# Moving the streamed tiles of two feed-forward layers to one place by the remainder of 512 bytes

## The chip, the cores and the metric

The kernel runs on one core of a Trainium2 chip. The metric is the device time of one execution in microseconds (us); the median of three runs stands for a kernel. TensorE does matrix products: a stationary operand of 128x128 words is loaded by a weight load (PEld in the profile), and then a moving operand, here called a stream, of up to 512 columns is sent through it by a matmul (PE). VectorE (DVE), ScalarE (ACT) and GpSimd (POOL) do the elementwise work, and SyncE (SP) issues the DMAs. SBUF is the working memory of 128 partitions; an address in this text is a byte offset inside a partition, the same in all of them.

## The reference

```python
def mab(q, kv):
    s = scale * (q @ kv.transpose(0, 2, 1))
    s = s - s.max(-1, keepdims=True)
    a = np.exp(s)
    a /= a.sum(-1, keepdims=True) + 1e-09
    return a @ kv
h = mab(I, x)                      # 32 inducing rows against 12480 tokens of 128
x = mab(x, h)
h = x @ w_in;  x = np.maximum(0.01 * h, h) @ w_out          # layer 1, d_ff 2048
h = x @ w_in2; x = (h / (1 + np.exp(-1.702 * h))) @ w_out2  # layer 2, d_ff 2048
```

Everything is float32: x is 12480x128, the weights are 128x2048 and 2048x128.

## The kernel before

The tokens are cut into 25 tiles: 23 of 512 tokens and, last in each layer, two of 352. Attention comes first, in about 45 us, with the weights' conversion beside it. Then `steps` (L799) runs layer 1 and layer 2, tile after tile, 16 steps to a tile; a step is one block of 128 of the 2048 hidden units. The order on each engine is the order in which the code issues the work (`manual_schedule`, L105); tokens of layer 2 follow those of layer 1 without a pause.

To keep float32 accuracy at the speed of the fp32r type, an operand is split into a high and a low half and the products are summed:

- `ffn_in`, layer 1 (L743): one matmul, stationary a 128-column slice of `hw`, stream `at`. Attention's last product is folded into `hw`, so that `at` holds the attention weights.
- `ffn_in`, layer 2 (L747 to L749): three matmuls, stationary slices of `w2h`, `w2l`, `w2h`, streams `x2h`, `x2h`, `x2l`.
- `ffn_act` (L757 to L765): the activation and the split of its result into `ghi` (ScalarE) and `glo` (VectorE). In layer 2 the Silu's result passes through a tile `g`.
- `ffn_out` (L775 to L777), both layers, three steps later (`LOOK`): three matmuls, stationary slices of `v1` or `v2`, streams `ghi`, `ghi`, `glo`. At a tile's end layer 1 adds one more, L779, with stationary `lin` and stream `at`.

So a step has 4 matmuls in layer 1 (65 to a tile, with L779) and 6 in layer 2 (96 to a tile), and each has a weight load of its own, which runs while the matmul ahead of it streams.

Where the tiles lie: the pools `const`, `slots`, `wts` and `conv` are allocated one after the other and stay; the pool `main` (L501) is opened where the pools of the attention were, and takes its tags in the order of their first use, each buffer rounded up to a multiple of 32 bytes. A first tile of `main`, `gap` (L505), is never written or read; it only takes room. In the program before, all the stationary operands of the layers (`hw`, `w2h`, `w2l`, `v1`, `v2`, `lin`, slices of 512 bytes) start at addresses that leave 416 when divided by 512. `main` starts at a remainder of 416 too, and behind `gap`'s 448 bytes and 5248 bytes of small tiles (`nmx`, `na`, `nsum`, `rows`) follow `at`, `ghi` and `glo`: 416 + 448 + 5248 leaves 480. Two tiles of 64 bytes (`mxt`, `sst`) and others of whole multiples of 512 lie between these and `x2h`, which so starts at 480 + 128, remainder 96:

| tile | operand of | remainder of 512, before | from the stationary operands' place |
|---|---|---|---|
| `hw`, `v1`, `v2`, `w2h`, `w2l`, `lin` | stationary | 416 | 0 |
| `at`, `ghi`, `glo` | stream | 480 | 64 above |
| `x2h`, `x2l` | stream, layer 2 alone | 96 | 192 above |
| `g`, `o_t` | no matmul | 96 | 192 above |

All buffers of the streams are 2048 bytes, a multiple of 512, so that every buffer of a tag has the same remainder.

Of the kernel before, what the change touches and what calls it, by code (L numbers as in the profile page):

```python
# [10 lines left out]
F32 = mybir.dt.float32  # L11
# [7 lines left out]
P = 128  # L19
# [38 lines left out]
def kernel(  # L58
# [442 lines left out]
    main = ctx.enter_context(tc.tile_pool(name="main", bufs=2))  # L501
    ps_a = ctx.enter_context(tc.tile_pool(name="ps_a", bufs=2, space=PSUM))


    main.tile([P, 112], F32, tag="gap", name="gap", bufs=1)  # L505

    def halves(src, name, pool=const, tag=None):
        shape = list(src.shape)
        hi = pool.tile(shape, F32R, name=f"{name}h", tag=f"{tag or name}h")
        lo = pool.tile(shape, F32R, name=f"{name}l", tag=f"{tag or name}l")  # L510
        nc.scalar.activation(out=hi, in_=src, func=AF.Copy)
        nc.vector.tensor_tensor(out=lo, in0=src, in1=hi.bitcast(F32), op=ALU.subtract)  # L512
        return hi, lo
# [333 lines left out]
    def late_matrix(make, src, name, args, first):  # L847
        def begin():
            late[name], parts = make(src, name, *args)
            for k, part in enumerate(parts):  # L850
                stages = convert_stages(*part)
                n = first + 16 * k
                at(n + 1, stages[0])
                for j, stage in enumerate(stages[1:]):
                    at(n + 6 + 4 * j - (n + 6) % 4 + 2, stage)
        at(first, begin)

    late_matrix(matrix_in, moe2_w_in, "w2", ["w"], 60)
    late_matrix(matrix_out, moe2_w_out, "v2", [], 160)

    def split_x2(t):
        x2h_t[t] = halves(x2_t.pop(t), "x2", main)

    for t in range(NT):
        at(NT * NF + (t - 1) * NF + 6, split_x2, t)
# [51 lines left out]
```

## Time and profile before

| what | us |
|---|---|
| median of 3 runs (972.02 to 972.75) | 972.42 |
| the profiled execution, by the clock of the runs | 971.38 |
| its span, first to last instruction | 969.2 |
| TensorE matmul busy | 957.5 |
| ScalarE busy | 783.6 |
| VectorE busy | 633.7 |

The profiled execution lies 1.04 us (0.1%) below the median, and 2.2 us of it lie outside the span. A matmul's record overlaps the next one's, so the busy share says how much of the time some matmul was in flight; how fast they follow one another is read from their starts. In the profile a line such as `acc<-ghi,v` names the tile written, then those read.

### The profile page before, as it was taken

The numbers are of one execution on the slowest core, as the hardware profiler recorded it, in microseconds if no ns is written. First come the engines' busy times: TensorE is split into PE (matmuls) and PEld (weight loads), VectorE is DVE, ScalarE is ACT, GpSimd is POOL, SyncE is SP. The second block draws the span as 40 slices with busy tenths as digits, with TensorE's granted clock in tenths as the row PEclk, the third lists the DMA queues.
The fourth block names the chain that finished last, engine by engine and source line by source line (L and its number), as shares of the span: only waits on it lengthen the run. The fifth ranks groups of instructions, "written<-read, shape, count | busy, mean of one in ns | idle before, by whom it ended". The sixth has DMA issues, their size and how long they took to land.

```text
span 969.2 us, 13231 instructions
## 1 busy us (share of the span) xinstructions
PE 957.5 (99%) x4590; PEld 781.5 (81%) x4590; DVE 633.7 (65%) x1008; ACT 783.6 (81%) x1359; POOL 51.3 (5%) x63
## 2 busy tenths in 40 slices
PE   9889999999999999999999999999999999999998
PEld 7568787887878878898888888888888888888888
DVE  4778788878878777765555555555555555555555
ACT  6566677777767666689999999999999999999997
POOL 1311110201101000000000000000000000000000
PEclk9999999999999999999999999999999999999999
DMA  9202120031000100000000000000000000000000
GB/s 341 100 0 55 34 66 23 7 94 32 23 22 4 30 12 19 8 2 11 12 12 11 12 11 12 11 23 12 11 11 12 12 11 11 12 11 23 12 12 16
DMA packets 15433, 27.90 MB, mean 29 GB/s; under 512 B 2358, under 2 KB 6998, under 8 KB 15366
## 3 DMA queue, kind: packets, MB, share of 16 engines
q1 hardware_dynamic: 15366, 27.06, 8.7%
q8 instruction: 36, 0.59, 0.3%
q14 instruction: 31, 0.25, 0.1%
HBM read 14.79 MB, written 6.39 MB: 22 GB/s over the span
## 4 chain that ended last, share of the span: by engine, by line
PE 97%; DVE 2%; ACT 1%; POOL 0%; issue 0%; ACTq 0%; DVEq 0%
PE acc L777 19%; PE acc L776 18%; PE acc L775 18%; PE h_ps L749 9%; PE h_ps L743 9%; PE h_ps L747 9%; PE h_ps L748 9%; PE xT_ps L280 1%; PE idle_ps L118 1%; PE s_ps L599 1%; PE acc L779 1%; ACT e_t L311 0%; PE s_ps L295 0%; DVE mx L299 0%; DVE pT_t L339 0%
## 5 line engine op out<-in xcount | busy, mean ns | idle before, releaser
L765 DVE TENSOR_TENSOR glo<-g,ghi 128x512 fp32r<-128x512 f32 (+1 forms) x400 | 271.7, 679 | 239.2 <-ACT ghi L764 226.4
L757 ACT ACTIVATE ghi<-h_ps 128x512 fp32r<-128x512 f32 (+1 forms) x400 | 233.2, 588 | 99.7 <-PE h_ps L743 97.5
L758 DVE SCALAR_TENSOR_TENSOR glo<-h_ps,ghi 128x512 fp32r<-128x512 f32 (+1 forms) x400 | 264.8, 675 | 72.3 <-ACT ghi L757 67.2
L777 PE MATMUL acc<-glo,v 128*128 128x512 f32 (+1 forms) x800 | 309.9, 387 | 0.0
L776 PE MATMUL acc<-ghi,v 128*128 128x512 f32 (+1 forms) x800 | 309.0, 386 | 0.0
L775 PE MATMUL acc<-ghi,v 128*128 128x512 f32 (+1 forms) x800 | 308.1, 385 | 0.0
L763 ACT ACTIVATE g<-h_ps 128x512 f32<-128x512 f32 (+1 forms) x400 | 235.0, 587 | 35.8 <-PE h_ps L749 0.5
L764 ACT ACTIVATE ghi<-g 128x512 fp32r<-128x512 f32 (+1 forms) x400 | 248.2, 620 | 12.7
L776 PEld LDWEIGHTS acc<-ghi,v 128*128 128x128 f32 x800 | 150.3, 188 | 32.6
L777 PEld LDWEIGHTS acc<-glo,v 128*128 128x128 f32 x800 | 150.3, 188 | 30.2 <-DVE glo L758 0.4
L775 PEld LDWEIGHTS acc<-ghi,v 128*128 128x128 f32 x800 | 150.3, 188 | 28.6 <-issue 0.2
L749 PE MATMUL h_ps<-x2l,w2h 128*128 128x512 f32 (+1 forms) x400 | 156.8, 392 | 0.0
L743 PE MATMUL h_ps<-at,hw 128*128 128x512 f32 (+1 forms) x400 | 156.4, 391 | 0.4 <-ACT at L579 0.4
L747 PE MATMUL h_ps<-x2h,w2h 128*128 128x512 f32 (+1 forms) x400 | 154.7, 387 | 0.0
L748 PE MATMUL h_ps<-x2h,w2l 128*128 128x512 f32 (+1 forms) x400 | 153.1, 383 | 0.0
L743 PEld LDWEIGHTS h_ps<-at,hw 128*128 128x128 f32 x400 | 75.1, 188 | 20.1 <-issue 4.7
L748 PEld LDWEIGHTS h_ps<-x2h,w2l 128*128 128x128 f32 x400 | 75.1, 188 | 16.2
L749 PEld LDWEIGHTS h_ps<-x2l,w2h 128*128 128x128 f32 x400 | 75.1, 188 | 15.5
L747 PEld LDWEIGHTS h_ps<-x2h,w2h 128*128 128x128 f32 x400 | 75.1, 188 | 15.5
L793 ACT ACTIVATE x<-acc 128x512 f32<-128x512 f32 (+1 forms) x25 | 14.7, 587 | 7.6 <-PE acc L779 7.6
L796 DVE TENSOR_SCALAR o_t<-acc 128x512 f32<-128x512 f32 (+1 forms) x25 | 16.8, 670 | 0.5 <-PE acc L777 0.5
L512 DVE TENSOR_TENSOR x2l<-x,x2h 128x512 fp32r<-128x512 f32 (+1 forms) x25 | 16.8, 671 | 0.0
(108 smaller groups left out, 314.2 us busy)
## 6 DMA issues: line engine op xcount, KB each, us to landing
out_dram<-o_t SPq DMA_DIRECT2D x23, 256.0 KB, 2.0
xn<-in_x_dram SPq DMA_DIRECT2D x11, 512.0 KB, 10.1
raw<-in_moe_w_in_dram SPq DMA_DIRECT2D x8, 512.0 KB, 8.9
raw<-in_moe_w_out_dram SPq DMA_DIRECT2D x8, 512.0 KB, 4.4
at<-hlhi SPq DMA_DIRECT2D x42, 64.0 KB, 2.0
at<-hllo SPq DMA_DIRECT2D x42, 64.0 KB, 2.0
xn<-in_x_dram SPq DMA_DIRECT2D x2, 176.0 KB
out_dram<-o_t SPq DMA_DIRECT2D x2, 176.0 KB, 1.8
```

Source lines behind the costliest of these rows:

```text
L743: nc.tensor.matmul(o, hw[:, cols], at_t[t], start=True, stop=True)
L747: nc.tensor.matmul(o, wh[:, cols], hi, start=True, stop=False)
L748: nc.tensor.matmul(o, wl[:, cols], hi, start=False, stop=False)
L749: nc.tensor.matmul(o, wh[:, cols], lo, start=False, stop=True)
L757: nc.scalar.activation(out=hi, in_=o, func=AF.Relu)
L758: nc.vector.scalar_tensor_tensor(out=lo, in0=o, scalar=0.0, in1=hi.bitcast(F32), op0=ALU.max, op1=ALU.subtract)
L763: nc.scalar.activation(out=g, in_=o, func=AF.Silu, scale=BETA)
L764: nc.scalar.activation(out=hi, in_=g, func=AF.Copy)
L765: nc.vector.tensor_tensor(out=lo, in0=g, in1=hi.bitcast(F32), op=ALU.subtract)
L775: nc.tensor.matmul(o, v[:, f, 0, :], hi, start=(f == 0), stop=False)
L776: nc.tensor.matmul(o, v[:, f, 1, :], hi, start=False, stop=False)
L777: nc.tensor.matmul(o, v[:, f, 0, :], lo, start=False, stop=end)
```

## The change

`gap` shrinks from 112 words of 4 bytes to 88, from 448 to 352 bytes: everything behind it in `main` moves down by 96 bytes. When layer 2's first tile is split (`split_x2`, ahead of the first use of `x2h`), a second tile `gap2` of 96 words (384 bytes) is taken, once; `x2h`, `x2l`, `g` and `o_t` are allocated behind it. No instruction uses either gap.

```diff
-    main.tile([P, 112], F32, tag="gap", name="gap", bufs=1)
+    main.tile([P, 88], F32, tag="gap", name="gap", bufs=1)
...
+    gaps = []
+
     def split_x2(t):
+        if not gaps:
+            gaps.append(main.tile([P, 96], F32, tag="gap2", name="gap2", bufs=1))
         x2h_t[t] = halves(x2_t.pop(t), "x2", main)
```

Remainders after: `at`, `ghi`, `glo` 480 - 96 = 384; `x2h`, `x2l`, `g`, `o_t` 96 - 96 + 384 = 384. The stationary operands lie in pools ahead of `main` and stay at 416, so every stream of both layers starts 32 bytes below them by the remainder of 512.

## Rows read from the trace of the kernel before

**Rows 1.** Page, busy time and share of the span by engine.
```profile
PE 957.5 (99%) x4590; PEld 781.5 (81%) x4590; DVE 633.7 (65%) x1008; ACT 783.6 (81%) x1359; POOL 51.3 (5%) x63
```
**Rows 2.** Page, granted TensorE clock over 40 slices, 9 is 90% or more.
```profile
PEclk9999999999999999999999999999999999999999
```
**Rows 3.** Page, the chain of work that ended last, by engine and line.
```profile
PE 97%; DVE 2%; ACT 1%; POOL 0%; issue 0%; ACTq 0%; DVEq 0%
PE acc L777 19%; PE acc L776 18%; PE acc L775 18%; PE h_ps L749 9%; PE h_ps L743 9%; PE h_ps L747 9%; PE h_ps L748 9%; PE xT_ps L280 1%; PE idle_ps L118 1%; PE s_ps L599 1%; PE acc L779 1%; ACT e_t L311 0%; PE s_ps L295 0%; DVE mx L299 0%; DVE pT_t L339 0%
```
**Rows 4.** Stages: us, then busy us by engine, PEclk, DMA share, GB/s.
```profile
105.00:345.00 240.00, 240.00 (x1058) 194.20 (x1057) 194.50 (x307) 170.00 (x294) 29.31 (x28) 1.00 0.13 33
404.00:429.00 25.00, 25.00 (x150) 24.16 (x149) 18.29 (x35) 19.39 (x40) 0.00 (x0) 1.00 0.00 1
430.00:932.00 502.00, 502.00 (x2185) 409.98 (x2184) 278.99 (x409) 455.36 (x753) 0.00 (x0) 1.00 0.03 12
```
**Rows 5.** Timeline of TensorE, layer 1, L779 of two tiles: start us, us.
```profile
148.72 0.39 PE L779 MATMUL acc<-at,lin 128*128 128x512 f32 x1
...
163.59 0.40 PE L779 MATMUL acc<-at,lin 128*128 128x512 f32 x1
```
**Rows 6.** Timeline of TensorE, layer 2, L747 56 steps apart.
```profile
640.09 0.39 PE L747 MATMUL h_ps<-x2h,w2h 128*128 128x512 f32 x1
...
717.37 0.39 PE L747 MATMUL h_ps<-x2h,w2h 128*128 128x512 f32 x1
```
**Rows 7.** Timeline of TensorE, tiles of 352 columns, 13 matmuls apart.
```profile
419.83 0.32 PE L776 MATMUL acc<-ghi,v 128*128 128x352 f32 x1
...
421.91 0.32 PE L777 MATMUL acc<-glo,v 128*128 128x352 f32 x1
```
**Rows 8.** Groups of 430 to 930 us, by form: busy us, mean ns.
```profile
L749 PE MATMUL h_ps<-x2l,w2h 128*128 128x512 f32 x362 | 144.1, 398 | 0.0
L777 PE MATMUL acc<-glo,v 128*128 128x512 f32 x363 | 143.0, 394 | 0.0
L747 PE MATMUL h_ps<-x2h,w2h 128*128 128x512 f32 x363 | 142.4, 392 | 0.0
L776 PE MATMUL acc<-ghi,v 128*128 128x512 f32 x363 | 142.3, 392 | 0.0
L775 PE MATMUL acc<-ghi,v 128*128 128x512 f32 x363 | 141.6, 390 | 0.0
L748 PE MATMUL h_ps<-x2h,w2l 128*128 128x512 f32 x362 | 140.5, 388 | 0.0
```
**Rows 9.** The same view: VectorE and ScalarE in layer 2.
```profile
L765 DVE TENSOR_TENSOR glo<-g,ghi 128x512 fp32r<-128x512 f32 x363 | 251.4, 693 | 221.8 <-ACT ghi L764 209.4 <-PE h_ps L749 10.1 <-PE acc L776 0.5
L764 ACT ACTIVATE ghi<-g 128x512 fp32r<-128x512 f32 x363 | 229.1, 631 | 11.5
L763 ACT ACTIVATE g<-h_ps 128x512 f32<-128x512 f32 x363 | 217.2, 598 | 35.0
```
**Rows 10.** Groups of 105 to 345 us, by form: layer 1.
```profile
L758 DVE SCALAR_TENSOR_TENSOR glo<-h_ps,ghi 128x512 fp32r<-128x512 f32 x255 | 171.8, 688 | 43.4 <-ACT ghi L757 41.3
L757 ACT ACTIVATE ghi<-h_ps 128x512 fp32r<-128x512 f32 x255 | 151.3, 599 | 66.0 <-PE h_ps L743 64.2 <-DVE glo L758 0.6 <-DVE v L158 0.3
L743 PE MATMUL h_ps<-at,hw 128*128 128x512 f32 x255 | 100.1, 393 | 0.0
L776 PE MATMUL acc<-ghi,v 128*128 128x512 f32 x255 | 99.8, 391 | 0.0
```
**Rows 11.** Timeline of all engines in layer 2: a weight load beside a stream.
```profile
640.32 0.39 PE L748 MATMUL h_ps<-x2h,w2l 128*128 128x512 f32 x1
640.33 0.19 PEld L749 LDWEIGHTS h_ps<-x2l,w2h 128*128 128x128 f32 x1
...
640.55 0.40 PE L749 MATMUL h_ps<-x2l,w2h 128*128 128x512 f32 x1
```

## The prediction

> **What bounds the kernel now.** I read the shares of the page first: a matmul is in flight for 957.5 of 969.2 us, and no other engine is above 81% of the span [rows 1]. [...] The chain that ended last is TensorE for 97%, and within it the lines of the two layers, in proportion to how often they run [rows 3]. So the question is one number: how far apart two matmuls of a layer start. The stages say that this holds throughout: from 105 to 345 us (layer 1) and from 430 to 932 us (layer 2) TensorE is busy for the whole stretch, while VectorE has 194.5 of 240 us in the one and ScalarE 455.4 of 502 us in the other [rows 4].
>
> The starts give the interval. In layer 1 two L779, 65 matmuls apart, start 14.87 us apart: 228.8 ns per matmul [rows 5]. In layer 2 two L747, 56 steps of 6 matmuls apart, start 77.28 us apart: 230.0 ns, 1380 ns a step [rows 6]. A tile of 352 columns has 2.08 us for 13 matmuls, 160.0 ns [rows 7]. The six matmuls of a step of layer 2 are not alike: their durations go from 388 to 398 ns though all are 128x128 by 512 columns [rows 8]. Their mean is 392.3 ns and the mean interval 230.0 ns, so a record is some 162.3 ns longer than the interval that follows its start, and the six intervals are by that estimate 225.7 (L748), 227.7, 229.7, 229.7, 231.7 and 235.7 ns (L749). That spread is what speaks for this change having something to act on: equal work, 10 ns of difference. No other engine explains it. TensorE does not idle ahead of them [rows 8], and VectorE and ScalarE repeat the same work in every step [rows 9].
>
> **What the change moves.** It adds and removes no instruction; two tiles that nothing touches change size or appear, so the direct cost is nil. What moves are addresses. (1) `at`, `ghi` and `glo` go from 64 bytes above the stationary operands to 32 below, by the remainder of 512; (2) `x2h` and `x2l` go from 192 above to 32 below; (3) `g`, `o_t` and, in between, the softmax's tiles move too. All stationary operands stay. `main` shifts by 96 bytes over the rooms of closed pools, whose pieces are 2 to 8 KB; worked out from the sizes, each tile of the first stage still covers the same old pieces, so no wait is added or lost. No queue is passed and no DMA is added; those into `at` only land 96 bytes lower.
>
> For (3) I take nothing. Should ScalarE's two operations of a step of layer 2 become slower at the new places, 598 + 631 = 1229 ns of the step's 1380 leave 151 ns, 12% of their time, before ScalarE is the bound; VectorE has 693 of 1380 ns there [rows 9] and 688 of 915 ns in layer 1 [rows 10].
>
> For (1) and (2) the trace of before shows no pair at 32 below, so it is bounded. The weight load of the next matmul starts 10 ns after the stream that it runs beside (640.33 against 640.32 us) and lasts 0.19 us of that stream's 0.23 [rows 11]: both read SBUF at the same time for most of it, and the distance between their start addresses is what the change sets. Two distances are seen. With 64 bytes alone (layer 1) the interval is 228.8 ns. In layer 2 the streams at 192 bytes are those of L747, L748, L749, by the durations 229.7, 225.7 and 235.7 ns, mean 230.4; and one kind next to another gives a step of 230.0 on average. So the distance, or what follows from it, moves the interval by ns, and it does so in both directions.
>
> [...]
>
> The terms, on 21 tiles of layer 1 (the first two wait for other engines in part and are left out), 21 x 65 = 1365 intervals, 23 x 96 = 2208 of layer 2 and 130 + 192 = 322 of the four short tiles. *Upper bound of the ordinary case*: everything runs as the distance nearest to the new one, 64 bytes (it is 96 bytes off, the other 224): layer 1 keeps its 228.8, layer 2 gets it too: 2208 x 1.2 ns = 2.6 us gained. *Lower bound*: everything runs as the shortest interval seen, 225.7: 1365 x 3.1 + 2208 x 4.3 + 322 x about 3 ns = 4.2 + 9.5 + 1.0 = 14.7 us gained. I take the middle, 227.3 ns, because both seen distances are multiples of 64 bytes and the new one is the first that is not, so that there is no reason to stay with the value of either: 1365 x 1.5 + 2208 x 2.7 + 322 x 1.5 = 2.0 + 6.0 + 0.5 = **8.5 us gained**. What is late next: nothing. A step of layer 2 would last 1364 ns against ScalarE's 1229, and of layer 1 909 ns against VectorE's 688. On the profiled execution, 971.4 us with its span of 969.2 and 2.2 around it, that gives 962.9; the median of the runs is 1.0 us higher and the same sum on it gives 963.9 us.
>
> **The rivals.** *Nothing happens.* The 10 ns spread comes from the order of the matmuls or from their results' places, not from SBUF addresses, and the change does not do what it is about: 972.4 us. For it: within layer 1, where all streams have one distance, L743 and L776 still differ by 2 ns in their means [rows 10], and only TensorE's own reads are in question. Against it: the 388 of L748 and the 398 of L749 are the same in the mean over 362 steps, so they are tied to something fixed.
>
> *The cost of meeting disappears.* If 32 below is a distance at which stream and load hardly meet, the part of the interval that does not grow with the columns goes. From 352 to 512 columns layer 1 pays 228.8 - 160.0 = 68.8 ns for 160 columns, 0.43 ns each, or 220.2 ns for 512: 8.6 ns an interval in layer 1, 9.8 in layer 2 and 8.6 in the short tiles, 11.7 + 21.6 + 2.8 = 36 us: 936 us. Against it: no matmul of the six comes near 220 ns. [...]
>
> *It becomes slower.* The load starts 10 ns behind its stream. With the stream 64 above, it starts ahead of the load's place and runs away from it; 32 below, it starts behind it and has to pass it, so the two meet where now they part. The place is every interval of both layers. Priced at 231.7 ns, the second slowest of the six now: 1365 x 2.9 + 2208 x 1.7 + 322 x 2 = 4.0 + 3.8 + 0.6 = 8.4 us lost, 980.8 us; at the slowest one, 235.7, it would be 9.4 + 12.6 + 2 = 24 us and 996. It decides from a mean interval over 229.6 on, where the gain of layer 2 no longer pays for the loss of layer 1. For it: the largest interval, 235.7, belongs to a stream of other distance than the rest. Against it: it follows an interval of 225.7 at that same distance, so that distance is not slow as such.
>
> **How the numbers follow.** Forecast, some ns gained per interval (957.7 to 969.8 us): 0.44. Most of the cost gone (below 957.7): 0.15. No change: 0.17. Slower: 0.24. About 0.2% is what a measurement of this kernel can tell from no change, and the chances go by it: faster 0.44 + 0.15 = 0.59, same 0.17, slower 0.24. The time is that of the likeliest case, 963.9. The range has to reach to both unlikely sides: down to 945 us, some way beyond the shortest interval towards the rival of 936, and up to 981 us, the slower rival's price. Below it I leave about 0.08 and above it about 0.1. The forecast's own range is 957.7 to 969.8.
>
> **What would show it.** In the trace of after: L747 56 steps apart is under 77.28 us, 76.4 if the forecast holds (75.8 at 225.7, 77.9 at 231.7); the two L779 are 14.77 us apart rather than 14.87; the short tiles have under 160 ns. The six durations of layer 2 should lie closer together than 388 to 398, as all streams now have one distance. If they keep their spread line by line and the interval is 230.0, the addresses don't matter. If layer 2 falls to 228.8 and layer 1 stays, the mixture was all there was to gain. ScalarE's 598 and 631 ns should stay; if they grow, (3) was wrongly put at nothing. The prediction is wrong if an interval at 32 below exceeds 229.6 ns, since no other term can pay for it.

## The result: slower by 1.4%

| kernel | median us | ratio to before | 95% interval |
|---|---|---|---|
| before | 972.59 | 1 | |
| after | 986.56 (985.47 to 987.46) | 1.0139 | 1.0127 to 1.0152 |

The program of after issues the same instructions in the same order on every engine. Its page, shares and chain:

```profile
PE 972.7 (99%) x4590; PEld 782.8 (79%) x4590; DVE 635.4 (64%) x1008; ACT 783.7 (80%) x1359; POOL 51.0 (5%) x63
PE 96%; DVE 1%; ACT 1%; DMA 1%; POOL 0%; issue 0%; SPq 0%; ACTq 0%; DVEq 0%
```

Some matmul is in flight for 99% of the span, as before [rows 1], and TensorE carries the chain as it did [rows 3]. VectorE and ScalarE work hardly longer than before (635.4 us against 633.7, 783.7 against 783.6). The time lies between the matmuls. The timeline of TensorE in after, two L779 of neighbouring tiles in layer 1 and two L747 of layer 2, 55 steps apart (start us, us):

```profile
152.68 0.40 PE L779 MATMUL acc<-at,lin 128*128 128x512 f32 x1
...
167.85 0.40 PE L779 MATMUL acc<-at,lin 128*128 128x512 f32 x1
...
640.70 0.40 PE L747 MATMUL h_ps<-x2h,w2h 128*128 128x512 f32 x1
...
717.70 0.40 PE L747 MATMUL h_ps<-x2h,w2h 128*128 128x512 f32 x1
```

Two numbers follow from these rows: 15.17 us for 65 intervals, 233.4 ns, where before had 228.8 [rows 5]; and 77.00 us for 330, 233.3 ns, where before had 230.0 [rows 6]. Both layers now run at the same interval. The groups of 430 to 930 us by form say the same (busy us, mean ns):

```profile
L764 ACT ACTIVATE ghi<-g 128x512 fp32r<-128x512 f32 x354 | 223.7, 632 | 11.2
L763 ACT ACTIVATE g<-h_ps 128x512 f32<-128x512 f32 x355 | 212.0, 597 | 41.1
L748 PE MATMUL h_ps<-x2h,w2l 128*128 128x512 f32 x355 | 140.6, 396 | 0.0
L749 PE MATMUL h_ps<-x2l,w2h 128*128 128x512 f32 x355 | 140.2, 395 | 0.0
L747 PE MATMUL h_ps<-x2h,w2h 128*128 128x512 f32 x355 | 140.2, 395 | 0.0
L775 PE MATMUL acc<-ghi,v 128*128 128x512 f32 x352 | 139.4, 396 | 0.0
```

Six unlike durations, 388 to 398 ns [rows 8], have become 395 and 396; ScalarE's two moved by 1 ns at most [rows 9]. The sum: 1365 intervals of layer 1 x 4.5 ns + 2208 of layer 2 x 3.3 ns = 6.1 + 7.3 = 13.4 us. The two traces agree: from the fourth step of the third tile to the last matmul, after takes 13.3 us longer. The first two tiles of layer 1 add 130 x 4.5 ns = 0.6 us by estimate, which gives 14.0; the medians differ by 14.0 too, and the ratio of 1.0139 comes to 13.5. The short tiles stayed at 160 ns.

The spans of the two profiled executions differ by 16.1 us. The other 2.7 us arise ahead of 63 us and do not belong to the change. The timeline of TensorE in before, in after and in the kernel with the second gap alone (an experiment below, which is faster than before): layer 1's first matmul, and a later matmul of the weights' preparation between those of layer 1's first two tiles:

```profile
45.14 0.50 PE L743 MATMUL h_ps<-at,hw 128*128 128x512 f32 x1 [0.36 <-ACT at L579]
60.33 1.02 PE L672 MATMUL hw_ps<-w,hT 128*128 128x512 f32 x2
```

```profile
46.19 0.50 PE L743 MATMUL h_ps<-at,hw 128*128 128x512 f32 x1 [0.36 <-ACT at L579]
63.02 1.02 PE L672 MATMUL hw_ps<-w,hT 128*128 128x512 f32 x2
```

```profile
46.11 0.50 PE L743 MATMUL h_ps<-at,hw 128*128 128x512 f32 x1 [0.36 <-ACT at L579]
62.87 1.02 PE L672 MATMUL hw_ps<-w,hT 128*128 128x512 f32 x2
```

And the stretch from 54 to 57 us in the same three (us, then busy us of PE, PEld, DVE, ACT and POOL, the granted clock, DMA share, GB/s):

```profile
54.00:57.00 3.00, 3.00 (x18) 1.55 (x17) 2.99 (x6) 1.20 (x2) 0.00 (x0) 1.00 0.00 0
```

```profile
54.00:57.00 3.00, 3.00 (x9) 2.36 (x8) 1.92 (x4) 1.62 (x3) 0.00 (x0) 0.53 0.00 0
```

```profile
54.00:57.00 3.00, 3.00 (x9) 2.36 (x8) 2.01 (x4) 1.54 (x3) 0.00 (x0) 0.51 0.00 0
```

After's layer 1 starts 1.05 us later than before's, and another 1.64 us come up to this L672: from 54 to 57 us the granted clock averages 0.53, where before's trace has 1.00. TensorE had been idle for 2.6 us just ahead; so it had in before's trace, and there the clock did not fall. The kernel with the second gap alone lost about as much in both places and is still faster than before. Runs of either kernel go both ways: of after's four, the two with a mean granted clock of 1.000 took 985.5 and 985.9 us and the two with 0.998 took 987.3 and 987.5, and of before's 15 beside the last experiments three had 1.000 and twelve 0.998. From 85 us on the clock of after is 1.00, so that it has no part in the 13.3 us.

### The profile page after: what moved, and what is told of

Same layout as the page of the kernel before. It is cut to its first block, busy times and chain, and to the rows that moved or that the text cites. A ratio compares the mean times of both kernels' runs of the same rounds, so it can differ in the third digit from the quotient of the medians.

```text
span 985.3 us, 13231 instructions
## 1 busy us (share of the span) xinstructions
PE 972.7 (99%) x4590; PEld 782.8 (79%) x4590; DVE 635.4 (64%) x1008; ACT 783.7 (80%) x1359; POOL 51.0 (5%) x63
## 4 chain that ended last, share of the span: by engine, by line
PE 96%; DVE 1%; ACT 1%; DMA 1%; POOL 0%; issue 0%; SPq 0%; ACTq 0%; DVEq 0%
PE acc L776 19%; PE acc L777 18%; PE acc L775 18%; PE h_ps L743 9%; PE h_ps L747 9%; PE h_ps L749 9%; PE h_ps L748 9%; PE xT_ps L280 1%; DMA xn<-in_x_dram 1%; PE s_ps L599 1%; PE acc L779 1%; ACT e_t L311 0%; PE s_ps L295 0%; DVE mx L299 0%; ACT xT L284 0%; PE s_ps L533 0%
## 5 line engine op out<-in xcount | busy, mean ns | idle before, releaser
L757 ACT ACTIVATE ghi<-h_ps 128x512 fp32r<-128x512 f32 (+1 forms) x400 | 233.2, 587 | 107.2 <-PE h_ps L743 105.5
L758 DVE SCALAR_TENSOR_TENSOR glo<-h_ps,ghi 128x512 fp32r<-128x512 f32 (+1 forms) x400 | 265.8, 675 | 78.2 <-ACT ghi L757 74.1
L775 PE MATMUL acc<-ghi,v 128*128 128x512 f32 (+1 forms) x800 | 312.4, 391 | 0.0
L776 PE MATMUL acc<-ghi,v 128*128 128x512 f32 (+1 forms) x800 | 312.0, 390 | 0.0
L748 PE MATMUL h_ps<-x2h,w2l 128*128 128x512 f32 (+1 forms) x400 | 156.0, 390 | 0.0
L747 PE MATMUL h_ps<-x2h,w2h 128*128 128x512 f32 (+1 forms) x400 | 155.7, 389 | 0.0
L749 PE MATMUL h_ps<-x2l,w2h 128*128 128x512 f32 (+1 forms) x400 | 155.5, 389 | 0.0
L748 PEld LDWEIGHTS h_ps<-x2h,w2l 128*128 128x128 f32 x400 | 75.1, 188 | 17.0
L749 PEld LDWEIGHTS h_ps<-x2l,w2h 128*128 128x128 f32 x400 | 75.2, 188 | 16.5
L747 PEld LDWEIGHTS h_ps<-x2h,w2h 128*128 128x128 f32 x400 | 75.2, 188 | 16.4
L793 ACT ACTIVATE x<-acc 128x512 f32<-128x512 f32 (+1 forms) x25 | 14.7, 587 | 8.0 <-PE acc L779 8.0
## 6 DMA issues: line engine op xcount, KB each, us to landing
xn<-in_x_dram SPq DMA_DIRECT2D x11, 512.0 KB, 10.7
```

Of the source, the lines that this page charges most:

```text
L747: nc.tensor.matmul(o, wh[:, cols], hi, start=True, stop=False)
L748: nc.tensor.matmul(o, wl[:, cols], hi, start=False, stop=False)
L749: nc.tensor.matmul(o, wh[:, cols], lo, start=False, stop=True)
L757: nc.scalar.activation(out=hi, in_=o, func=AF.Relu)
L758: nc.vector.scalar_tensor_tensor(out=lo, in0=o, scalar=0.0, in1=hi.bitcast(F32), op0=ALU.max, op1=ALU.subtract)
L775: nc.tensor.matmul(o, v[:, f, 0, :], hi, start=(f == 0), stop=False)
```

## The experiments

From here on "distance" is how far a stream's address lies above the address of the stationary operands, by the remainder of 512 bytes. Before has 64 for `at`, `ghi`, `glo` and 192 for `x2h`, `x2l`; after has 480 (32 below) for all. Intervals in tables of the scans are means of the starts' differences within one tile, from its fourth step on. In layer 2 they end where the tile's last step begins, so that all streams have the distance named. In layer 1 they run on to the tile's L779, with three matmuls of the next tile among them; without those, 0 has 227.2 ns and 64 has 229.1 to 229.2.

**Many distances in one run.** Buffers grow by 512 bytes and a stream starts in its buffer where the tile's number says:

```diff
+    def placed(tag, at, base, n, bufs):
+        o = (at - base) % 512 // 4
+        return main.tile([P, TOK + P], F32R, tag=tag, name=tag, bufs=bufs)[:, o : o + n]
...
-        hi = main.tile([P, TOK], F32R, tag="ghi", name="ghi", bufs=LOOK + 2)[:, : tok[t]]
+        hi = placed("ghi", OUT_AT[l][t], 64, tok[t], LOOK + 2)
```

and likewise for `glo`, `at`, `x2h` and `x2l`; `base` is the distance at offset 0.

> Every buffer of at, ghi, glo, x2h and x2l is 512 bytes longer, and a token tile's streams start at an offset in it that the tile's number sets, so that one run shows many distances from the stationary operands by the remainder of 512: in layer 1 tiles 2 to 17 have 0, 32, 64 ... 480 bytes, in layer 2 the same tiles have them in the opposite order; tiles 18 to 21 have 64 and 480 in turn, and tile 22 has 256. Theory 'distance': the interval follows the distance, so all tiles at 64 have about 228.9 ns, all at 480 (32 below) 233.3 ns, in either layer and wherever they stand, and the other distances have values of their own between some 225 and 236 ns. Rival 'other tiles': what the change moved besides the streams (g, o_t, the small tiles, which stay as before here) made it slower; then all tiles of a layer show the interval of before, 228.8 ns in layer 1 and about 230 in layer 2. Rival 'mixture of layers': the interval is a matter of how streams of two distances alternate; then layer 2, which has one distance per tile here, differs from layer 1 at the same distance by no more than layer 1's tiles differ among themselves.

Layer 2 of this run, L757 (before's L747) 8 steps of 6 matmuls apart, in five tiles with distances 480, 160, 64, 32 and 0, in this order:

```profile
478.40 0.40 PE L757 MATMUL h_ps<-x2h,w2h 128*128 128x512 f32 x1
489.60 0.40 PE L757 MATMUL h_ps<-x2h,w2h 128*128 128x512 f32 x1
...
523.14 0.40 PE L757 MATMUL h_ps<-x2h,w2h 128*128 128x512 f32 x1
534.39 0.40 PE L757 MATMUL h_ps<-x2h,w2h 128*128 128x512 f32 x1
...
768.43 0.39 PE L757 MATMUL h_ps<-x2h,w2h 128*128 128x512 f32 x1
779.41 0.39 PE L757 MATMUL h_ps<-x2h,w2h 128*128 128x512 f32 x1
...
790.48 0.39 PE L757 MATMUL h_ps<-x2h,w2h 128*128 128x512 f32 x1
801.68 0.39 PE L757 MATMUL h_ps<-x2h,w2h 128*128 128x512 f32 x1
...
812.82 0.40 PE L757 MATMUL h_ps<-x2h,w2h 128*128 128x512 f32 x1
823.71 0.39 PE L757 MATMUL h_ps<-x2h,w2h 128*128 128x512 f32 x1
```

11.20, 11.25, 10.98, 11.20 and 10.89 us for 48 intervals: 233.3, 234.4, 228.8, 233.3 and 226.9 ns. All tiles:

| distance | layer 1, ns | layer 1 at 256 more, ns | layer 2, ns | layer 2 at 256 more, ns |
|---|---|---|---|---|
| 0 | 228.1 | 228.1 | 227.2 | 227.2 |
| 32 | 232.8 | 232.8 | 233.3 | 233.3 |
| 64 | 229.5 | 229.5 | 229.1 | 229.0 |
| 96 | 233.6 | 233.6 | 233.3 | 233.3 |
| 128 | 231.9 | 231.9 | 232.4 | 232.4 |
| 160 | 234.0 | 234.0 | 234.2 | 234.2 |
| 192 | 233.2 | 233.2 | 233.2 | 233.2 |
| 224 | 233.2 | 233.2 | 233.4 | 233.2 |

The distance sets the interval, in either layer and wherever the tile stands; the rival of the other tiles (`g`, `o_t`) falls, since they kept their remainder here, and the two layers agree within 1 ns at every distance, so the layer itself counts for little. Two things are more than was expected. The values repeat with 256, not 512. And every odd multiple of 32 lies at 232.8 ns or above: 32 below is one of them (224 by the remainder of 256). One tile broke the rule: of layer 2's two tiles at 64 among the last five, one ran at 228.9 and the first, after a tile at 0, at 233.3. So one distance can have two steady patterns.

> As the scan in steps of 32 bytes, but with steps of 4: layer 1's tiles 2 to 22 stand 0, 4, 8 ... 80 bytes above the stationary operands, layer 2's 64 bytes below to 16 above. Theory 'distance' with whole groups of 32 or 64 bytes: the interval is flat within a group and jumps at 32 or 64 (228.9 ns at 64, 233.3 at 32 below). The same theory without groups: it moves with every 4 bytes, a step of some 1.7 ns or less. Rival 'other tiles': flat throughout, 228.8 and 230 ns.

| distance, layer 1 | 0 | 4 | 8 | 12 | 16 | 20 | 24 | 28 | 32 | 36 | 44 | 60 | 64 | 68 |
|---|---|---|---|---|---|---|---|---|---|---|---|---|---|---|
| ns | 228.0 | 236.3 | 233.3 | 229.5 | 231.6 | 236.1 | 233.6 | 227.4 | 233.4 | 234.8 | 230.5 | 227.3 | 229.8 | 239.3 |

| bytes below, layer 2 | 64 | 60 | 52 | 44 | 36 | 32 | 28 | 20 | 8 | 4 | 0 |
|---|---|---|---|---|---|---|---|---|---|---|---|
| ns | 233.2 | 233.3 | 231.2 | 238.6 | 230.0 | 233.3 | 236.7 | 226.7 | 230.1 | 226.7 | 226.8 |

There are no groups of 32 or 64 bytes: 4 bytes move the interval by up to 9.5 ns (64 to 68), so the step of 1.7 ns that was expected at most is refuted too. Nothing runs faster than 226.7.

> The scan in steps of 4 bytes goes on: layer 1's tiles 2 to 22 stand 84 to 164 bytes above the stationary operands, layer 2's tiles 2 to 7 at 168 to 188; its tiles 8 to 22 repeat distances already seen (4, 20 and 36 below, 0, 12, 28, 44, 60, 256) in another order, some of them twice in a row. Theory 'distance by the remainder of 256': no value lies far under the 226.7 ns seen 4 and 20 bytes below; the repeated ones come back to within 0.5 ns where they had one value (226.7 at 4 and 20 below, 227.2 at 0 and 256, 227.3 at 60), and 64 at the start of a tile may settle at another value when the tile ahead had another distance, as it did once (233.3 for 228.9). Rival 'chance of the order': the repeated distances come back more than 2 ns off.

Layer 1 from 84 to 164 bytes gives 227.8 (156) to 239.4 ns (132). The repeated ones in layer 2: 0, 256, 28, 60 and 4 below come back to 226.7 to 227.2 each time, 4 below three times; 12 and 44 to 229.0 and 230.0, where layer 1 had 229.5 and 230.5; but 20 below, which gave 226.7 in the scan before and once here, gave 228.9 in two tiles one after the other, behind one at 4 below: 2.2 ns off, which was the rival's sign, for this one distance. So distances keep their values, save for some with two patterns, and none comes under 226.7.

**Streams of `ffn_in` alone.** `OUT_AT` stays at 64 for all tiles.

> As the scan in steps of 32 bytes, but only the streams of ffn_in (at in layer 1, x2h and x2l in layer 2) change their distance; ghi and glo stay 64 above throughout. If each matmul's interval follows its own stream's distance, layer 1's tiles move by a quarter of what the full scan shows (one stream of four) and layer 2's by half. If it is the sequence that counts, tiles at 192 in layer 2 give the 230.0 ns of before, as they are before's own mixture, and others don't lie between the two pure values.

| in layer 2: `x2h`, `x2l` at | 64 | 192 | 480 | 0 | 32 | 160 |
|---|---|---|---|---|---|---|
| ns, `ghi` and `glo` at 64 | 228.9 | 230.0 | 230.0 | 232.8 | 232.2 | 234.4 |
| ns, all at that distance | 229.1 | 233.2 | 233.3 | 227.2 | 233.3 | 234.2 |

The sequence counts, not each matmul by itself. No mixture lies half-way between its two pure values, as it would if each stream brought its own interval; 32 and 480 lie between them all the same, which was not expected. 0 and 64 are the two best of the table alone and give 232.8 mixed, worse than either. The value of before, 230.0, is that of its own mixture, 64 and 192, and lies under the half-way between them.

**The stationary operands moved.** The first scan with, in addition:

```diff
+    wts.tile([P, 40], F32, name="ahead", tag="ahead")
...
-    main.tile([P, 112], F32, tag="gap", name="gap", bufs=1)
+    main.tile([P, 72], F32, tag="gap", name="gap", bufs=1)
```

> The full scan in steps of 32 bytes with the stationary operands moved: 160 bytes are put ahead of w1, so hw, v1, v2, w2h and w2l start at a remainder of 64 and no longer 416, and the first gap is 160 bytes smaller, so that every stream keeps the address it has in the scan. Theory 'distance': the picture of the scan moves by 160 bytes, so a tile that is named d there is 160 nearer now: the tiles named 224 (now 64) have 228.9 ns, those named 128 (now 32 below) 233.3. Rival 'place': the remainder of the stream's own address counts, whatever the stationary operand's; then each tile has the interval that it has in the scan, 228.9 at those named 64 and 233.3 at those named 480.

Two tiles of layer 2 of this run, named 416 (distance 256 now) and 64 (distance 416 now), L758, 8 steps apart:

```profile
526.87 0.40 PE L758 MATMUL h_ps<-x2h,w2h 128*128 128x512 f32 x1
537.76 0.39 PE L758 MATMUL h_ps<-x2h,w2h 128*128 128x512 f32 x1
...
771.67 0.40 PE L758 MATMUL h_ps<-x2h,w2h 128*128 128x512 f32 x1
782.91 0.40 PE L758 MATMUL h_ps<-x2h,w2h 128*128 128x512 f32 x1
```

10.89 and 11.24 us: 226.9 and 234.2 ns, where the tiles of those names, at the same addresses, had 234.2 and 229.1 in the first scan. By the new distances, 0 and 160 by the remainder of 256, they are where they should be, and so are 18 others of layer 2's 23 long tiles (224 - 160 = 64: 229.1; 128 - 160, 32 below: 233.4). The other three, all named 480 (distance 320, or 64 by the remainder of 256), ran at 233.3 instead of 229.1. That is what their place had given in the first scan, but also the second pattern of 64: each of them follows a tile at 160 here. In layer 1 a tile named 480 came to 229.1, as 64 does. So it is the distance, not the stream's place.

**The cost by itself.** 704 matmuls at the end of before, with the other engines idle but for two operations of VectorE at the start:

```diff
...
+    stream = late["v2"].rearrange("p f h c -> p (f h c)")
+    wh = late["w2"][0]
+    for width in (128, 64, 32):
+        for at in (0, 4, 32, 64, 160, 480, 508):
+            for k in range(32):
+                o = (k % 4) * 512 + at // 4
+                nc.tensor.matmul(
+                    alone[:width], wh[:, (k % NF) * P : (k % NF) * P + width],
+                    stream[:, o : o + 512], start=True, stop=True,
+                )
+    for k in range(32):
+        nc.tensor.matmul(alone, idle[:, :P], idle, start=True, stop=True)
```

> The kernel before, with 704 matmuls more at its end, which write an unused PSUM tile: in 21 blocks of 32 the stream is 512 columns of v2 and the stationary operand a slice of w2h of 128, then 64, then 32 columns, at distances of 0, 4, 32, 64, 160, 32 below and 4 below; the last 32 stream the bf16 tile idle. Other engines are nearly idle then. [...] Rival 'other engines': without ScalarE's and VectorE's traffic all blocks come down to some 216 ns. [...] The bf16 block, whose stream has half the bytes, should be near 216 ns.

The timeline merges equal lines, so that a row is the start of the first of a stretch, the time from it to the end of the last, and their number. Rows of the blocks 128 wide at 0, 4 and 64, 64 wide at 4, 32 wide at 0 and 4, and bf16:

```profile
967.71 6.07 PE L886 MATMUL alone<-v,w2h 128*128 128x512 f32 x26
974.80 6.08 PE L886 MATMUL alone<-v,w2h 128*128 128x512 f32 x25
989.82 6.12 PE L886 MATMUL alone<-v,w2h 128*128 128x512 f32 x26
1026.14 7.04 PE L886 MATMUL alone<-v,w2h 128*64 128x512 f32 x29
1071.11 6.65 PE L886 MATMUL alone<-v,w2h 128*32 128x512 f32 x28
1078.29 6.37 PE L886 MATMUL alone<-v,w2h 128*32 128x512 f32 x26
1123.30 5.77 PE L891 MATMUL alone<-idle 128*128 128x512 bf16 x26
```

Less the last record's own 0.38 to 0.40 us and divided by one less than their number, they give 227, 237, 229, 237, 232, 239 and 216 ns. By all starts but each block's first four (ns):

| stationary columns | 0 | 4 | 32 | 64 | 160 | 32 below | 4 below |
|---|---|---|---|---|---|---|---|
| 128 | 227.1 | 237.1 | 233.4 | 228.9 | 234.3 | 233.3 | 230.1 |
| 64 | 230.2 | 237.3 | 230.8 | 228.4 | 233.5 | 231.9 | 229.1 |
| 32 | 231.6 | 239.0 | 232.6 | 231.9 | 231.0 | 229.9 | 229.4 |

The rival of the other engines falls: with VectorE and ScalarE idle and 128 stationary columns the picture of the scan is there, save that 4 below has 230.1 where the scans had 226.7. The bf16 block is at 216 ns, the value that the expectation names without a run behind it; no fp32r block came down to it. Over those 216 the fp32r blocks lie by 11.1 to 21.1 ns with 128 columns, 12.4 to 21.3 with 64 and 13.4 to 23.0 with 32: this excess neither halves with 64 columns nor quarters with 32, so it is not a price on the bytes that the load reads. Which distances are the slow ones does change with the load: with 32 columns, 32 below falls from 233.3 to 229.9 ns and 0 rises from 227.1 to 231.6, so that their order turns round. The bf16 block has a stationary operand in bf16 as well, and it was run at one distance, so it does not tell which of the two operands matters.

**Which load, and how long a stream.**

```diff
...
+    def block(w, at, n=512):
+        for k in range(32):
+            o = (k % 4) * 512 + at[k % len(at)] // 4
+            c = (k % 8) * P + w[k % len(w)] // 4
+            nc.tensor.matmul(
+                alone[:, :n], wh[:, c : c + P], stream[:, o : o + n], start=True, stop=True
+            )
+
+    for a in (32, 4, 160):
+        block([0, a], [0, a])
+        block([0, a], [a, 0])
+    for n in (512, 508, 504, 496, 480, 448, 384, 256):
+        for at in (0, 32, 64):
+            block([0], [at], n)
```

> The kernel before with 960 matmuls more at its end, in 30 blocks of 32, whose output nothing uses. First six blocks: stationary operands and streams each alternate between two places, 0 and a, with a = 32, 4 and 160. In the first block of a pair each matmul has its stream at the distance 0 from its own stationary operand, and the load that runs beside that stream, the next matmul's, stands a bytes off; in the second block the stream is at 0 from the operand that is loaded beside it and a bytes off its own. Theory 'the load beside the stream': the second blocks run at 227 ns, the first at some 233 (a = 32), 232 to 237 (4) and 233 (160). Theory 'own operand': the other way round. Then streams of 512, 508, 504, 496, 480, 448, 384 and 256 columns at distances 0, 32 and 64. [...]

The pairs don't decide: with the stream at 0 from its own operand, or from the one loaded beside it, a = 32 gave 231.8 and 231.6 ns, a = 4 gave 233.5 and 233.1, a = 160 gave 233.9 and 229.8. The lengths tell more. Rows of 480 columns at 32, 384 at 0, and 256 at 0:

```profile
1105.65 5.66 PE L887 MATMUL alone<-v,w2h 128*128 128x480 f32 x25
1139.84 3.45 PE L887 MATMUL alone<-v,w2h 128*128 128x384 f32 x19
1155.75 2.80 PE L887 MATMUL alone<-v,w2h 128*128 128x256 f32 x22
```

By all starts but each block's first four (ns), and the differences from distance 0:

| columns | at 0 | at 32 | at 64 | 32 less 0 | 64 less 0 |
|---|---|---|---|---|---|
| 512 | 227.4 | 233.3 | 228.9 | 5.9 | 1.5 |
| 508 | 227.6 | 230.4 | 226.7 | 2.8 | -0.9 |
| 504 | 227.0 | 226.7 | 228.9 | -0.3 | 1.9 |
| 496 | 223.3 | 224.4 | 226.7 | 1.1 | 3.4 |
| 480 | 216.7 | 220.0 | 218.1 | 3.3 | 1.4 |
| 448 | 202.7 | 206.7 | 200.0 | 4.0 | -2.7 |
| 384 | 173.3 | 173.3 | 173.3 | 0 | 0 |
| 256 | 120.0 | 117.8 | 117.8 | -2.2 | -2.2 |

What a distance costs against 0 goes up and down with the length and does not grow steadily along the stream: 32 costs 5.9 ns at 512 columns, saves 0.3 at 504, costs 4.0 at 448 and saves 2.2 at 256. 504 columns at 32 (226.7 ns) are as fast as 512 at 0 (227.4). At 384 columns the three distances make no difference at all (173.3 ns each). A cost paid all along the stream does not describe this; one at the change of operands fits better, and is not shown.

**One gap at a time, and a better place.** The second gap alone and both at 96 words differ from after in one number:

```diff
-    main.tile([P, 88], F32, tag="gap", name="gap", bufs=1)
+    main.tile([P, 112], F32, tag="gap", name="gap", bufs=1)
```

```diff
-    main.tile([P, 88], F32, tag="gap", name="gap", bufs=1)
+    main.tile([P, 96], F32, tag="gap", name="gap", bufs=1)
```

The first gap alone is before with 88 words and no second gap; four below is the scan's kernel with 508 for all tiles.

> The second gap alone: the first stays at 112 words, so at, ghi and glo stay 64 above the stationary operands and x2h and x2l come from 192 to 64 above. Theory 'distance': layer 1 keeps 228.9 ns and layer 2 falls from 230.0 to 228.9, 2208 x 1.1 ns = 2.4 us faster than before (0.25%). Rival 'second orbit': layer 2 settles where one tile of the scan did at 64 and runs at 233.3 ns, 7.3 us slower. Rival 'the second gap is what costs' (g and o_t at a new place): slower by the change's own 14 us.

> The first gap alone: 88 words and no second, so at, ghi and glo stand 32 below and x2h and x2l 96 above. Theory 'distance': layer 1 has the 233.3 ns of the changed kernel, layer 2 mixes two odd multiples of 32 and comes to about 233.3 too: slower by some 6 + 7 = 13 us, as the change is. Rival 'the gaps act together': clearly less than that.

> Both gaps of 96 words: every stream at the remainder of the stationary operands themselves, distance 0. Theory 'distance': layer 1 at some 228.0, layer 2 at 226.7 to 227.2 ns: 1495 x 0.9 + 2208 x 2.8 to 3.3 = 7.5 to 8.6 us faster than before, some 964 us. Rival 'order of the tiles': the scan's values at 0 held for one tile among others; in a kernel with nothing else layer 2 is no better than 228.9.

> Every stream 4 bytes below the stationary operands: buffers 512 bytes longer, all streams 127 words into or 79 words into them. Theory 'distance': 226.7 ns in both layers: 1495 x 2.2 + 2208 x 3.3 = 10.6 us faster, some 961 us. Rival 'two orbits': the 230.1 ns of the block without other work at that distance, so layer 2 as before, layer 1 slower by 1.8 us.

| kernel | distances | median us | ratio to before | 95% interval | layer 1, layer 2 ns |
|---|---|---|---|---|---|
| second gap alone | 64, 64 | 971.10 | 0.9974 | 0.9965 to 0.9983 | 228.9, 228.9 |
| first gap alone | 480, 96 | 987.48 | 1.0143 | 1.0127 to 1.0158 | 233.3, 233.3 |
| both gaps of 96 words | 0, 0 | 962.55 | 0.9890 | 0.9877 to 0.9904 | 226.8, 226.7 |
| four below | 508, 508 | 962.00 | 0.9882 | 0.9869 to 0.9896 | 226.7, 226.7 |

Before's median beside them was 972.83. Every one went as the distances said. By the medians: 2.4 us gain expected of the second gap and 1.7 measured, some 13 us loss of the first and 14.7 measured, 7.5 to 8.6 us gain at 0 and 10.3 measured, 10.6 four below and 10.8 measured. The ratios, which are not those of the medians, come to 2.5, 13.9, 10.7 and 11.5 us. At 0, layer 1 did better than the scan's table had it, whose means take in matmuls of the next tile at another distance. The two last differ by less than their intervals, so the plain one, both gaps of 96 words, is the version to keep: it is faster than both kernels. Its trace, two L779 and two L747 55 steps apart:

```profile
148.18 0.39 PE L779 MATMUL acc<-at,lin 128*128 128x512 f32 x1
162.91 0.39 PE L779 MATMUL acc<-at,lin 128*128 128x512 f32 x1
...
640.96 0.39 PE L747 MATMUL h_ps<-x2h,w2h 128*128 128x512 f32 x1
715.76 0.39 PE L747 MATMUL h_ps<-x2h,w2h 128*128 128x512 f32 x1
```

14.73 us for 65 intervals and 74.80 for 330: 226.6 and 226.7 ns.

## Why the prediction was wrong

- *What bounds the kernel*: right. The interval between matmuls is the whole story: 13.4 of the 14.0 us follow from it by the traces, the rest by the same interval as an estimate, and no other engine took part.
- *Parts without cost, and (3)*: right. No instruction, wait or queue changed, ScalarE's operations stayed at 597 and 632 ns, and the scans, which leave `g` and `o_t` at their remainder, show the streams alone to matter.
- *That the distance has something to act on*: right, and shown by moving the stationary operands under streams that stayed. The six intervals worked out from the durations were also right: by all starts of layer 2 in before's trace they run from 225.8 ns (behind L748) to 235.9 (behind L749). But unlike durations are no sign of unlike distances; they belong to a pattern over several matmuls. The kernel with the second gap alone has one distance, 64, for all streams, and its six durations of layer 2 repeat in threes (430 to 930 us, by form):

```profile
L747 PE MATMUL h_ps<-x2h,w2h 128*128 128x512 f32 x364 | 143.4, 394 | 0.0
L775 PE MATMUL acc<-ghi,v 128*128 128x512 f32 x363 | 143.0, 394 | 0.0
L749 PE MATMUL h_ps<-x2l,w2h 128*128 128x512 f32 x364 | 142.7, 392 | 0.0
L777 PE MATMUL acc<-glo,v 128*128 128x512 f32 x363 | 142.3, 392 | 0.0
L748 PE MATMUL h_ps<-x2h,w2l 128*128 128x512 f32 x364 | 141.2, 388 | 0.0
L776 PE MATMUL acc<-ghi,v 128*128 128x512 f32 x363 | 140.8, 388 | 0.0
```

So the 225.7 ns of one interval was no price of one pair, and nothing that was tried ran a whole layer below 226.7.
- *The step that failed*: the interval at the new distance. The prediction took 227.3 ns for 32 below, between 225.7 and 228.8. Measured: 233.3, so that its size and the sign of the change were both wrong. The bracket was of one sign, though the same rows held 235.7 as an upper end, which went to the rival instead. And the reason for the middle, that both distances seen were multiples of 64 bytes and the new one was not, only said that nothing was known; the scan shows that all eight odd multiples of 32 are at 232.8 or above. With no row for such a distance, the sum had no ground for either sign.
- *The rival "slower"*: right in its sign and in the point from which it decides (an interval over 229.6 ns). Its price was 8.4 us at 231.7 ns; at the 233.3 measured it is 14, and the range went no further up than that price. Its mechanism, a stream that starts behind its load and has to pass it, was not borne out: 32 above, where the stream starts ahead as it does at 64, ran at 233.3 too, and what 32 costs against 0 does not grow steadily along the stream (5.9 ns at 512 columns, none at 384).
- *The rival "nothing happens"*: refuted, since distances alone move the interval from 226.7 to 239 ns. Whether the two operands meet, and where, no run here tells.
- *The rival "the cost disappears"*: its 220.2 ns rested on a slope from 352 to 512 columns. Streams alone show that the interval does not grow evenly: at 64, layer 1's distance, it goes up by 18.1 ns from 448 to 480 columns and by 10.8 from 480 to 512, so two lengths give no slope to go by. The bf16 block ran at 216 ns, and no fp32r stream of 512 columns was steady below 226.7.
- *What would show it*: the six durations did draw together (395 and 396), as was said of streams of one distance, but not because of the one distance: at 64 they stay at 388 to 394. The sign of being wrong that was named, an interval over 229.6 ns, is what came. "The mixture was all there was to gain" was tried alone: 0.26% by the second gap with 64 kept.

What stays open is the mechanism: why fp32r matmuls of 512 columns start 11 to 23 ns further apart than the bf16 block's 216, why the distance counts by the remainder of 256, and whether a stream's own operand or the one loaded beside it is the partner.

## What to carry to other kernels

Where TensorE is never idle, the addresses of stream and stationary operand are worth a scan, since here they moved the interval between fp32r matmuls of 512 columns from 226.7 to 239.4 ns. Buffers with some room and an offset that changes from tile to tile show dozens of places in one run. Look for one distance for all streams, since a mixture of two good ones can be worse than either (0 and 64 in layer 2: 232.8 ns mixed, 227.2 and 229.1 alone). And where the trace shows no row for a new placement, the bounds are those of all placements seen, to both sides, and the forecast has no sign.

## What the runs showed of the hardware

- With the same instructions, at a granted clock of 0.998 to 1.000 in the mean of a run, fp32r matmuls of 512 columns, each with a load of 128 columns, followed one another at 226.7 to 239.4 ns, depending on the distances; with both operands bf16, at the one distance tried, at 216.
- 4 bytes can cost 9.5 ns (64 to 68 bytes: 229.8 to 239.3), and the values repeat with 256 bytes: 0 and 256, 32 and 288 and so on agree within 0.1 ns in layer 1.
- Many steady intervals average to whole or simple multiples of 6.67 ns: 226.67 are 34 of them, 230.0 are 34.5, 233.33 are 35, and 228.89 are 34 and a third. In the lengths, 173.3, 200.0, 206.7, 216.7, 220.0, 223.3 and 120.0 ns are such numbers again (26, 30, 31, 32.5, 33, 33.5 and 18); the 234.2 ns at 160 is not one. It looks as if starts kept to steps of that size; no run shows why.
- Some distances have two steady patterns (64: 228.9 and 233.3; 20 below: 226.7 and 228.9; 4 below: 226.7 in the layers, 230.1 in the block by itself). In the scans the one found went with the tile ahead: 64 in layer 2 ran at 233.3 behind a tile at 0 or 160, and near 229 behind one at 96 or 480.
- The short tiles of layer 2 (352 columns) move with the distance too: 160.0 ns at 64 and 32 below, 161.1 at 0, 157.8 four below.
